# A fused attention and gated MLP kernel: the head and the first two chunks rewritten as one listed order

## The chip, the core and the metric

The kernel runs on one core of one Trainium2 chip. Its time is the device time of one execution in microseconds (us). Before the change it is 250.87 us, the median of three runs (250.81 to 252.08). The engines are called as in the profile: PE (matrix multiply), PEld (its weight loads), DVE (vector), ACT (activations), POOL and SP; POOL and SP also issue transfers (DMA).

## What is computed

Four batches of eight heads, 768 positions, 64 values a head. The positions form eight blocks of 96. A small matrix per head is normalized five times by rows and columns (Sinkhorn) and mixes the blocks of k and v; attention then runs inside each block, and its result goes through an MLP with the gate h cos h.

```python
P = sort_net
for _ in range(5):
    P = P - np.max(P, axis=-1, keepdims=True)
    P = np.exp(P)
    P = P / (np.sum(P, axis=-1, keepdims=True) + 1e-09)
    P = P / (np.sum(P, axis=-2, keepdims=True) + 1e-09)
k_sorted = np.einsum('bhij,bhjcd->bhicd', P, k_b)
v_sorted = np.einsum('bhij,bhjcd->bhicd', P, v_b)
scores = scale * np.matmul(q_b, k_sb.transpose(0, 1, 2, 4, 3))
attn = softmax(scores)
x = np.matmul(attn, v_sb)          # (3072, 512) after reordering
h = x @ w_in                       # (3072, 2048)
out = (h * np.cos(h)) @ w_out      # (3072, 512)
```

## The kernel before

**Tiling.** The 3072 rows of the result are worked in eight chunks of 384 rows; chunk n holds half of batch n // 2, that is four blocks (u = 0 to 3). Sinkhorn works on two groups of two batches, one group in 128 partitions. Batches 0 and 1 make up group 0.

**Steps of a chunk.** Each block goes through `qk` (eight score matmuls into one PSUM tile, then a maximum, L454, and a subtraction, L455, on DVE), `expo` (L479 on ACT), a transpose of the probabilities p (`p_transpose`, L503 on PE, or by DMA from SP's queue, L490), `av` (eight matmuls, L516, a reciprocal and a product on DVE, L523 and L525) and `x_transpose` (L541). Then `moe_up` runs eight `up` calls (16 feature tiles of 128, L553, cosine on ACT L557, gate product on DVE L560), and `moe_down` runs three row tiles of 16 matmuls each into an accumulator (L570), copies them out and stores them. Score groups, sorts and transposes of the following chunk are placed in slots between these calls, written out by hand for each chunk.

**Sorting.** k and v are multiplied on PE by a block-diagonal matrix made from Sinkhorn's result (`bd`, spread at L274). `k_sort_0` sorts batch 0 for one half of its blocks, `k_sort_1` batch 1. `v_sort_b` needs v with the value index outermost; half of batch 0's columns are read straight from the loaded tile `kv`, the others after a permuting copy on POOL (`v_permute`, L177) into `vperm`.

**Memories.** PSUM has two pools: "big" with three tiles of two banks (B in the code) and "acc" with two tiles of one bank (C). Every score, sort, up and down result needs one of these tiles and holds it until ACT or DVE has read it.

**Order.** Each engine works its instructions in the order in which the code writes them. POOL's queue carries all loads of q, k, v and the weights beside memsets and permutes; SP's queue carries the small swaps of k halves (`k_swap`), transposes by DMA and most stores. Before, the head runs like this: sort_net is loaded; q for chunk 0, k and v of batch 0 are requested (L195 to L197); both Sinkhorn groups run in step for four iterations (L311 to L337), with chunk 0's query transposes and three weight loads between them; then batch 0's first half is sorted and chunk 0's four blocks are worked (L609 to L636). Chunk 0's up pass runs in two halves of 192 rows (L651 to L659). Batch 0's second half and batch 1 are sorted in slots of chunk 0's up and down passes and of chunk 1's up pass. From chunk 1's down pass on (L702) the work is the same in both versions.

**Keeping the PE busy.** `keep_warm` (L216) issues matmuls on a zero tile of 256 columns whose result nobody reads: 16 at the start, then three at a time between Sinkhorn steps.

Of the kernel before, what the change touches and what calls it, by code (L numbers as in the profile page):

```python
# [10 lines left out]
FP32 = mybir.dt.float32  # L11
# [3 lines left out]
AX = mybir.AxisListType  # L15


@with_exitstack
def kernel(
# [42 lines left out]
    gp = ctx.enter_context(tc.tile_pool(name="gp", bufs=9))  # L62
# [14 lines left out]
    ident = const.tile([128, 128], BF16, name="ident")  # L77

# [22 lines left out]
    QR, NQ = 4, 3  # L101

    QZ = IC * H2 * 2 * D
    q_mem = const.tile([blk, 2 * (QZ + D)], BF16, name="q_mem")
    q_rows = q_mem[:, :H * QR * D].rearrange("p (h x) -> p h x", h=H)
# [10 lines left out]

    def load_q(n):  # L120
        b, ih = n // 2, n % 2
        if n < NQ:

            nc.gpsimd.dma_start(
                out=q_rows, in_=q[b][:, ih * IC * blk:(ih + 1) * IC * blk].rearrange(
                    "h (p r) d -> p h (r d)", r=QR))
# [40 lines left out]
    def v_permute(rows, lo=0, halves=True):  # L167

        for z in range(lo, D, VQ):
            dst = vperm[rows, :CD].rearrange("p (d c) -> p d c", d=D)[:, z:z + VQ]
            src = vv[rows, z:z + VQ, :blk]
            if halves:
                dst = dst.rearrange("p d (x t) -> p d x t", x=2)
                src = src.rearrange("p d (t x) -> p d x t", x=2)
            nc.gpsimd.tensor_copy(dst, src)  # L177

# [7 lines left out]
    kT, kT2 = [kTs[:, :, 0], kTs[:, :, 2]], kTs[:, :, :2]  # L186

    make_identity(nc, ident[:])
    NP = 3
    p_bufs = []  # L190
    for i in range(NP):
        t = const.tile([blk, 2 * H2, 128], BF16, name=f"p_buf{i}")
        nc.gpsimd.memset(t[:, :, blk:], 0.0)
        p_bufs.append(t)
    load_q(0)  # L195
    load(kbuf, 64, kin_d[0])
    load(vbuf, 0, vin_d[0])  # L197
# [6 lines left out]
    ones(0)  # L204
# [3 lines left out]
    warm = const.tile([128, 128], BF16, name="warm")  # L208
    nc.vector.memset(warm[:], 0.0)
    nc.vector.memset(vperm[:, CD:], 0.0)  # L210
    nc.vector.memset(kbuf[:64, :32 * D], 0.0)
# [16 lines left out]
    L = [const.tile([128, 2 * H, nb], FP32, name=f"L{g}") for g in range(NG)]  # L228
# [5 lines left out]

    for g in range(NG):
        nc.vector.reduce_max(nmx[g][:], P_a[:, g], axis=AX.X, negate=True)
        nc.scalar.activation(
            E[g][:], P_a[:, g], AF.Exp, bias=nmx[g][:], accum_out=cs[g][:])
# [13 lines left out]
    def product(lhs, rhs):  # L252
        ps = acc.tile([128, nb], FP32, name="sk", tag="acc")
        nc.tensor.matmul(
            ps[:], lhs.rearrange("p x j -> p (x j)"), rhs[:], start=True, stop=True)
        return ps

    for g in range(NG):
        nc.vector.reciprocal(ci[g][:], cs[g][:])
        nc.vector.scalar_tensor_tensor(  # L260
            L[g][:], rows_of, ci[g][:], along(E[g]), op0=ALU.mult, op1=ALU.mult)
    sk = [product(L[g], maskj) for g in range(NG)]
    keep_warm(3)
    nc.vector.tensor_copy(same[:], rows_of)
    nc.vector.tensor_copy(
        maskp.rearrange("p (b e x) -> p b e x", b=2, e=2),
        maskh.rearrange("p (b x e) -> p b e x", b=2, e=2))
# [18 lines left out]
    def q_turn(n, z, pool, tag):  # L286

        ps = pool.tile([128, 2, IC, QR, blk // QR], BF16, name="qps", tag=tag)  # L290
        for e in range(2):
            for hp in range(2):
                for r in range(QR):
                    nc.tensor.transpose(
                        ps[hp * D:(hp + 1) * D, e, :, r],
                        q_rows[:, (z * 2 + e) * 2 + hp, r * D:(r + 1) * D], ident[:blk, :blk])

        def place(hp, rows):
            dst = q_of(n, hp)[rows, :QW].rearrange("d (i h c) -> d h i c", h=H2, c=blk)
            return dst[:, z * 2:z * 2 + 2], ps[rows].rearrange("d e i r p -> d e i (r p)")  # L300

        if n == 0:
            return [place(0, slice(0, 128))]
        return [place(hp, slice(hp * D, (hp + 1) * D)) for hp in range(2)]

    def q_transpose(n, z, engs, pool, tag):
        for eng, (dst, src) in zip(engs, q_turn(n, z, pool, tag)):
            copy_on(eng, dst, src)

    held = const.tile([128, 1], FP32, name="held")  # L310
    for it in range(4):  # L311
        for g in range(NG):
            nc.scalar.activation(E[g][:], T[g][:], AF.Exp, scale=ci[g][:])
        if it > 1:
            copy_on(A, *turned[0])
        sk = [product(same, E[g]) for g in range(NG)]
        if it in (1, 2):
            turned = q_turn(0, it - 1, big, "big")
        keep_warm((3, 0, 0, 3)[it])
        if it == 1:  # L320

            nc.gpsimd.tensor_copy(held[:], cs[1][:])
            for z in range(3):
                load_w_in(z)
            v_permute(slice(0, 64), D // 2, False)
        elif it == 2:
            load_w_in(3)
            load_q(1)
            for z in range(4):
                load_w_out(z)  # L330
        for g in range(NG):
            nc.vector.reciprocal(rr[g][:], sk[g][:])
            nc.vector.tensor_tensor_reduce(
                T[g][:], E[g][:], rr[g][:], 1.0, 1e-9, ALU.mult, ALU.add, cs[g][:])
            nc.vector.reciprocal(ci[g][:], cs[g][:])
            if it == 3:
                spread(g)  # L337

    nc.vector.tensor_copy(
        order.rearrange("k (p r) -> k p r", r=QR),  # L340
        ident[:blk, :blk].rearrange("k (r p) -> k p r", r=QR))

    MH = H2 * IC
# [5 lines left out]
    def k_sort_0(ih, t0, nt, eng, pool, tag):  # L349

        ps = pool.tile([128, nt, 2 * MH], FP32, name="ks", tag=tag)
# [3 lines left out]
        ms, ts = slice(ih * MH, (ih + 1) * MH), slice(t0, t0 + nt)  # L355
        psv = ps.rearrange("p t (e m) -> p e m t", e=2)
        for hp in range(2):
            for x in range(2):
                copy_on(eng, kT[0][hp * D:(hp + 1) * D, hp + x, ms, ts],
                        psv[x * D:(x + 1) * D, hp])  # L360

    def k_sort_1(t0, eng, pool, tag):
        ps = pool.tile([128, 8, 2 * NB], FP32, name="ks", tag=tag)
# [3 lines left out]
        copy_on(eng, kT[1][:, ::2, :, t0:t0 + 8], ps.rearrange("p t (e m) -> p e m t", e=2))  # L367

    def k_sort_g(t0, eng, pool, tag):
        ps = pool.tile([128, 4, 4 * NB], FP32, name="ks", tag=tag)  # L370
# [10 lines left out]

    def keys_of(n, u, h2, hp):
        g, b2, ih = where(n)
        z = slice(hp, hp + 2)
        if n < 2:
            return kT[0][:, z, ih * MH + h2 * IC + u]
        m = h2 * nb + ih * IC + u
        return kT[1][:, z, m] if g == 0 else kT2[:, z, b2, m]

    def scores(out, n, u, h2, hp):  # L390
        x = (u * H2 + h2) * blk
        if n == 0:
            rows = slice(hp * D, (hp + 1) * D)
            nc.tensor.matmul(
                out[:blk], q_of(0, 0)[rows, x:x + blk], keys_of(n, u, h2, hp)[rows],
                start=True, stop=True)
        else:

            nc.tensor.matmul(  # L399
                out, q_of(n, hp)[:, x:x + 128], keys_of(n, u, h2, hp), start=True, stop=True)  # L400


    bdv = const.tile([128, 2 * H, nb], BF16, name="bdv")

    def v_turn():
        ps = big.tile([128, 128], FP32, name="bdp", tag="big")
# [4 lines left out]
        nc.scalar.copy(bdv.rearrange("p x i -> p (x i)"), ps[:])  # L411

    def v_cols(d, permuted):
        return vperm[:, d * blk:d * blk + 128] if permuted else vv[:, d]

    def v_sort_b(b, d0, nd, eng, pool, tag):
        ps = pool.tile([128, nd, 2 * NB], FP32, name="vs", tag=tag)


        rows, xs = slice(0, 64 + b * 64), slice((1 - b) * H, (2 - b) * H)  # L420
        for t in range(nd):
            nc.tensor.matmul(  # L422
                ps[:, t], v_cols(d0 + t, b == 1 or d0 + t >= D // 2)[rows],
                bdv[rows, xs].rearrange("p x i -> p (x i)"), start=True, stop=True)
        copy_on(
            eng, vS[0][:, b * 2 * NB:(b + 1) * 2 * NB, d0:d0 + nd],
            ps[:blk].rearrange("p t n -> p n t"))

    def v_sort_g(d0, nd, eng, pool, tag):
        ps = pool.tile([128, nd, 4 * NB], FP32, name="vs", tag=tag)  # L430
# [15 lines left out]
    def qk_part(n, u, part, pool, tag):  # L446
# [360 lines left out]
```

## Time and profile before

| What | Value |
|---|---|
| time, median of three runs (lowest to highest) | 250.87 us (250.81 to 252.08) |
| span of the profiled execution, first to last instruction | 248.0 us |
| PE busy | 231.1 us (93%) |
| DVE busy | 175.8 us (71%) |
| ACT busy | 157.3 us (63%) |
| POOL busy | 88.2 us (36%) |
| mean granted PE clock | 0.945 |
| sorting matrix of group 0 starts being spread | 12.66 us |
| first up matmul (chunk 0) | 29.20 us |
| first down matmul (chunk 0) | 51.96 us |
| first up matmul of chunk 1 | 70.72 us |
| HBM read, written | 27.27 MB, 6.29 MB |

The profiled execution's own time is not listed; the span stands for it, and what lies around the span is taken from the median time. Times inside the profile count from the start of the span. "Busy" of PE covers the whole flight of a matmul, so that a PE that is busy all the time need not be at its peak. The granted clock is the share of full speed that the chip's throttle lets the PE have at that time. In a listing by group, "idle before" names what ended the wait ahead of an instruction. A stage table gives busy time of each engine in a stretch of time, the number of instructions in brackets, then clock, share of the DMA engines and GB/s.

### The profile page before, as it was taken

The page shows a single profiled execution, that of the slowest core. Times are in us where ns is not written, and L with a number is a line of the kernel's source. Part 1 is how long each engine was busy: PE and PEld are TensorE (multiplying, and loading weights), DVE is VectorE, ACT ScalarE, POOL GpSimd, SP SyncE. Part 2 cuts the span into 40 slices and gives each one's busy share as a digit, 9 for nine tenths or more (in the row PEclk, how much of TensorE's full clock was granted, in tenths as well). Part 3 has the DMA queues.
Part 4 walks back from the last instruction along what each step waited for, and adds up shares of the span by engine and source line. Part 5 has one row for each costly group of instructions (what it writes and reads, how often), then busy time and mean ns, then how long its engine had stood idle before and what let it go on. Part 6 is the DMA issues. An engine that isn't in the chain of part 4 may idle for free.

```text
span 248.0 us, 5329 instructions
## 1 busy us (share of the span) xinstructions
PE 231.1 (93%) x2131; PEld 148.7 (60%) x2151; DVE 175.8 (71%) x322; ACT 157.3 (63%) x224; POOL 88.2 (36%) x104
## 2 busy tenths in 40 slices
PE   7887798878999999999999999999999999979994
PEld 5776696745566656665666556655565556435543
DVE  5579558897478876688568997898789759524710
ACT  4467846676568975789568866684667456634710
POOL 6369990799879707110353500800000000000000
PEclk9655569999999999999999999999999999999999
DMA  5999999895997058846897978937651650371012
GB/s 55 232 193 174 197 201 231 134 213 105 181 233 130 6 137 110 136 110 148 172 102 134 59 184 151 158 39 181 153 110 32 176 114 0 97 119 42 0 43 86
DMA packets 69001, 31.49 MB, mean 127 GB/s; under 512 B 57840, under 2 KB 64496, under 8 KB 68720
## 3 DMA queue, kind: packets, MB, share of 16 engines
q0 software_dynamic: 24048, 13.64, 40.8%
q1 hardware_dynamic: 43408, 15.28, 27.2%
q10 hardware_dynamic: 1520, 2.24, 2.8%
q8 instruction: 17, 0.28, 0.5%
q14 instruction: 8, 0.07, 0.1%
HBM read 27.27 MB, written 6.29 MB: 135 GB/s over the span
## 4 chain that ended last, share of the span: by engine, by line
PE 75%; DVE 10%; ACT 6%; DMA 5%; issue 2%; ACTq 0%; DVEq 0%; SPq 0%
PE h L553 32%; PE o L570 24%; PE sc L399 3%; PE av L516 3%; DMA vperm<-p_buf 2%; PE pps L503 2%; ACT p_buf L479 2%; DVE kTs L282 2%; PE ks L346 2%; PE vs L432 1%; DVE gg L560 1%; PE o L771 1%; DVE xn L525 1%; PE vs L422 1%; PE xps L541 1%
## 5 line engine op out<-in xcount | busy, mean ns | idle before, releaser
L553 PE MATMUL h<-xT,w_in_t 128*128 128x384 bf16 (+1 forms) x576 | 93.3, 313 | 2.1 <-DVE gg L560 0.8
L570 PE MATMUL o<-w_out_t,gg 128*128 128x512 bf16 x348 | 84.0, 379 | 1.6 <-DVE s L455 0.5
L557 ACT ACTIVATE c<-h,half_pi 128x768 f32<-128x768 f32 (+1 forms) x72 | 59.7, 830 | 36.2 <-PE h L553 33.9
L560 DVE TENSOR_TENSOR gg<-c,h 128x768 bf16<-128x768 f32 (+1 forms) x72 | 61.3, 859 | 25.2 <-ACT c L557 25.1
L553 PEld LDWEIGHTS <-w_in_t 128*128 128x128 bf16 x576 | 53.8, 100 | 29.7 <-issue 2.9
L570 PEld LDWEIGHTS <-gg 128*128 128x128 bf16 x368 | 33.6, 98 | 33.6 <-DVE s L455 0.7
L454 DVE TENSOR_REDUCE mx<-sc 96x4 f32<-96x384 f32 (+1 forms) x43 | 31.9, 741 | 3.2 <-PE sc L399 2.3
L455 DVE TENSOR_TENSOR s<-sc,mx 96x384 f32<-96x384 f32 (+1 forms) x43 | 32.2, 749 | 2.3
L177 POOL COPY vperm<-kv 64x1536 bf16<-64x1536 bf16 (+1 forms) x10 | 28.2, 2841 | 6.2 <-DMA kv<-in_v_dram 5.2
L479 ACT ACTIVATE p_buf<-s 96x768 bf16<-96x768 f32 x32 | 27.6, 894 | 2.4 <-ACT o_s L280 1.0
L280 ACT COPY o_s<-o 128x512 f32<-128x512 f32 (+1 forms) x18 | 10.3, 573 | 25.0 <-PE o L570 23.8
L525 DVE TENSOR_TENSOR xn<-av,r 96x512 bf16<-96x512 f32 x32 | 22.0, 686 | 1.1
L280 ACT CAST kTs<-ks 128x512 bf16<-128x512 f32 (+2 forms) x31 | 14.1, 456 | 6.2 <-PE ks L346 6.0
L134 POOL DMA_DIRECT2D kv<-in_q_dram x24 | 16.0, 675 | 3.1 <-DMA kv<-in_v_dram 2.2
L399 PE MATMUL sc<-kTs,q_turned 128*128 128x96 bf16 x224 | 16.1, 206 | 0.9 <-DVE s L455 0.7
L523 DVE RECIPROCAL r<-av 96x8 f32<-96x8 f32 x32 | 6.4, 199 | 14.7 <-PE av L516 14.6
L399 PEld LDWEIGHTS <-q_turned 128*128 128x128 bf16 x224 | 12.8, 98 | 4.8 <-DVE s L455 1.3
L282 DVE COPY o_s<-o 128x512 f32<-128x512 f32 (+1 forms) x7 | 4.5, 647 | 12.1 <-PE o L771 8.6
L557 ACT ACT_TABLE_LOAD x8 | 10.3, 1283 | 0.9 <-ACT o_s L280 0.7
L134 POOL DMA_DIRECT2D q_mem<-in_q_dram x16 | 10.6, 675 | 0.3 <-issue 0.3
L280 ACT CAST pair<-vs 96x512 bf16<-96x512 f32 (+1 forms) x12 | 8.7, 728 | 2.5 <-PE vs L432 2.0
L516 PEld LDWEIGHTS <-pT 96*128 96x128 bf16 (+1 forms) x160 | 7.8, 106 | 3.4 <-issue 1.2
(96 smaller groups left out, 212.8 us busy)
## 6 DMA issues: line engine op xcount, KB each, us to landing
out_dram<-o_s SPq DMA_DIRECT2D x15, 256.0 KB, 2.6
w_in_t<-in_moe_w_in_dram POOLq DMA_DIRECT2D x4, 512.0 KB, 10.6
w_out_t<-in_moe_w_out_dram POOLq DMA_DIRECT2D x4, 512.0 KB, 12.9
out_dram<-o_s ACTq DMA_DIRECT2D x8, 256.0 KB, 2.5
kv<-in_k_dram POOLq DMA_DIRECT2D x2, 768.0 KB, 13.3
kv<-in_v_dram POOLq DMA_DIRECT2D x2, 768.0 KB, 16.5
pair<-in_k_dram POOLq DMA_DIRECT2D x2, 768.0 KB, 11.5
kv<-in_v_dram POOLq DMA_DIRECT2D x6, 256.0 KB, 6.2
```

The source lines that it names most:

```text
L134: nc.gpsimd.dma_start(out=q_heads[:, i, :, e], in_=src[:, ih * IC + i, :, e])
L177: nc.gpsimd.tensor_copy(dst, src)
L280: eng.copy(dst, src)
L399: nc.tensor.matmul(out, q_of(n, hp)[:, x:x + 128], keys_of(n, u, h2, hp), start=True, stop=True)
L454: nc.vector.reduce_max(mx[:], scv, axis=AX.X)
L455: nc.vector.tensor_tensor(s_t[n, u][:, part[0]:part[0] + w], scv, mx.to_broadcast([blk, w, H2, blk]), op=ALU.subtract)
L479: nc.scalar.activation(dst, src, AF.Exp, scale=scale)
L525: nc.vector.tensor_tensor(xn.rearrange("p h e d -> p e h d"), avv[:, :, :, :D], r.to_broadcast([blk, 2, H2, D]), op=ALU.mult)
L553: nc.tensor.matmul(h[:, f2, :w], w_in_t[:, kk, f * 128:(f + 1) * 128], xT[n][:, kk, lo:hi], start=(kk == 0), stop=(kk == KC - 1))
L557: nc.scalar.activation(c[:, :, :w], h[:, :, :w], AF.Sin, bias=half_pi[:, 0:1])
L560: nc.vector.tensor_tensor(gt[n, fp][:, :, lo:hi], c[:, :, :w], h[:, :, :w], op=ALU.mult)
L570: nc.tensor.matmul(o[:], gt[n, f // 2][:, f % 2, ts * 128:(ts + 1) * 128], w_out_t[:, f, :], start=(f == 0), stop=(f == FC - 1))
```

## The change

Everything from the first load to the end of chunk 1's up pass is now one list of short calls (`ORDER`), worked from left to right; each call issues one step on one engine. The helpers are split so that a matmul group, its maximum, its subtraction or its eviction are calls of their own (`qm`, `qx`, `qs`; `vm`, `vc`; `um`, `uc`, `ug`; `dm`, `do`; `am`, `an`; `pp`, `pc`; `xt`, `xc`; `qt`, `qc`). The letter behind a call names the pool (B, C) or the engine (V for DVE, A for ACT, S for SP). `w` n puts n filler matmuls ahead of the next PSUM tile's own matmuls.

- q of both chunks of batch 0, k and v of batches 0 and 1 are requested ahead of all weights; q comes in halves (`load_q_half`), with two positions a piece in place of four, and chunk 1's q goes into the tile `pair`.
- Group 0's Sinkhorn iterations (`se`, `sp`, `sv` with second number 0) run ahead of group 1's, whose last two iterations move behind chunk 0's scores.
- Chunk 0's queries are transposed to both row halves: 64 transposes in place of 32. Its scores are 16 matmuls of 64 x 48 a block (one for each half of the keys) in place of eight of 64 x 96, and the sorted keys are written by three copies of 128 lanes (`k0c`) in place of sixteen of 64.
- Batch 0's second half of keys (`k4`, with a swap by DMA, `sw4`) and batch 1's keys (`k1`) are sorted in the head, ahead of and among chunk 0's scores.
- POOL's memsets and permutes stand between the weight loads (`zq1`, `one`, `zv`, `pv`).
- Chunk 0's up pass works four feature tiles of 192 rows in one PSUM tile, so that cosine and gate run on 768 elements instead of 384. Gate tiles hold two up calls each (five tiles in place of nine).
- Chunk 1's probabilities are transposed by DMA (`pd`), chunk 0's by PE.
- Fillers: 16 at the start as before, then 1, 6, 8, 8 and 3.

```diff
+ORDER = """
+se 0 0, sp 0 0, sv 0 0, se 1 0, lq 0 1, lk0, qt 0 0 0 2, qt 0 0 2 4, w 1, qt 0 0 4 6,
+qt 0 0 6 8, sp 1 0, qc 0 0 0 V, sv 1 0, se 2 0, qc 0 0 1 V, od, se 0 1, qt 0 1 0 8, sp 2 0,
+sv 2 0, qc 0 1 0 A, se 3 0, sp 0 1, lk1, sv 0 1, w 6, sp 3 0, w 8, se 1 1, qc 0 1 1 A, lv0,
+lq 1 1, sv 3 0, spr 0, lv1, lq 1 0, sp 1 1, k0 0 4 16 16 B, sv 1 1, k0c 0 4 16 16 A,
+k0 0 4 32 16 B, k0 0 4 0 16 B, k0c 0 4 32 16 A, se 2 1, k4 0 C, k1 32 B, k1 24 C,
+k0c 0 4 0 16 V, qm 0 0, k4c 0 A, k1 16 C, k1c 24 A, k1c 32 V, wi 0, wi 1, wi 2, wi 3, zq1,
+one 0, wo 0, zv, k1 8 C, k1 40 B, qx 0 0, qs 0 0, k1c 16 A, wo 1, qm 0 1, qx 0 1, qs 0 1,
+pv 0 2, pv 0 3, wo 2, pv 1 3, pv 1 2, wo 3, k1c 40 A, k1c 8 A, ex 0 0, k4 32 C, k4 16 C,
+vt, vtc A, k4c 32 A, k4c 16 A, qm 0 2, w 8, vm 0 0 8 24 8 C, qt 1 1 0 8, ex 0 1,
...
+vm 0 0 8 32 8 C, qc 1 1 0 V, qx 0 3, qs 0 3, vm 0 0 8 56 8 C, pp 0 0 B, w 3,
+vm 0 0 8 48 8 B, vm 0 0 8 40 8 B, pc 0 0 V, vc 0 0 8 48 8 V, pp 0 2 B, vc 0 0 8 32 8 A,
+vc 0 0 8 56 8 A, vc 0 0 8 40 8 A, pp 0 1 C, am 0 0, pc 0 2 V, ex 0 3, am 0 2, pc 0 1 A,
+an 0 0, an 0 2, sw4, pp 0 3 B, vm 1 0 8 48 8 C, pc 0 3 A, vc 1 0 8 48 8 A, am 0 1, k1 0 C,
+k1c 0 A, an 0 1, qm 1 3, qt 1 0 0 8, xt 0 2 C, qx 1 3, qs 1 3, xt 0 1 C, xc 0 2 A,
+xc 0 1 A, xt 0 0 C, am 0 3, sp 2 1, lk2 1, xc 0 0 A, vm 1 0 8 40 8 C, qm 1 2, sv 2 1,
+an 0 3, qx 1 2, qs 1 2, lk2 0, zp 0, zp 1, zp 2, pv 1 1, pv 1 0, lv2 3, lq 2 1, lv2 1,
+lv2 5, lv2 4, qc 1 0 0 V, lv2 2, qc 1 0 1 A, um 0 4 0 192, vc 1 0 8 40 8 A, se 3 1, ex 1 3,
+um 0 0 0 192, sp 3 1, vm 1 0 8 32 8 C, uc 0 4 0 192, um 0 2 0 192, vc 1 0 8 32 8 A, sv 3 1,
...
+do 0 2 V S, qh 2 0 0, um 1 0, uc 1 0, um 1 1, uc 1 1, ug 1 0, ug 1 1, spr 1, um 1 5,
+uc 1 5, ug 1 5, qh 2 0 1, qh 2 1 0, qh 2 1 1
+"""
...
+    def space(pool, shape, name, dtype=FP32):
+        pool, tag, banks = {"B": (big, "big", 2), "C": (acc, "acc", 1)}[pool]
+        if dtype == BF16 or not fill[0]:
+            return pool.tile(shape, dtype, name=name, tag=tag)
+
+        n = math.prod(shape[1:])
+        flat = pool.tile([128, 512 * banks], FP32, name=name, tag=tag)
+        for _ in range(fill[0]):
+            nc.tensor.matmul(flat[:, :256], warm[:], warm[:, :1].to_broadcast([128, 256]),
+                             start=True, stop=True)
...
+    def k0_mm(i0, ni, t0, nt, pool):
+        ps = ks[0, i0, t0] = space(pool, [128, nt, ni * H], "ks")
         for t in range(nt):
             k_products(ps, t, t0 + t, slice(64, 128),
-                       bds[0][64:, H:, ih * IC:(ih + 1) * IC])
...
+    def k0_out(i0, ni, t0, nt, eng):
+        copy_on(eng, kT0[:, 0, i0 * H:(i0 + ni) * H, t0:t0 + nt],
+                ks.pop((0, i0, t0)).rearrange("p t m -> p m t"))
...
+        qf = q_turned[n][:, u // U2]
+        for j in range(H):
+            w = (u % U2 * H + j % H2 * 2 + j // H2) * blk
+            for x in range(2):
+                rows = slice(x * D, (x + 1) * D)
+                nc.tensor.matmul(
+                    sc[:, x, j * HT:(j + 1) * HT], qf[rows, w:w + 128],
+                    kT0[rows, n, u * H + j], start=True, stop=True)
...
+    def up_mm(n, fp, lo=0, hi=TC):
+
+        w = hi - lo
+        z = TC // w
+        h = h_t[n, fp, lo] = space("B", [128, 2, 512], "h")
+        for f2 in range(2 * z):
+            f = fp * 2 + f2
+            for kk in range(KC):
+                nc.tensor.matmul(
+                    h[:, f2 // z, f2 % z * w:(f2 % z + 1) * w],
+                    w_in_t[:, kk, f * 128:(f + 1) * 128], xT[n][:, kk, lo:hi],
+                    start=(kk == 0), stop=(kk == KC - 1))
...
+    for call in ORDER.replace("\n", " ").split(","):
+        name, *args = call.split()
+        calls[name](*(named[a] if a in named else int(a) if a.isdigit() else a for a in args))
```

More of the change, by code (lines that the diff above doesn't have):

```diff
@@ L165, with v_permute @@
     VQ = 16
[L167 to L177, printed above, removed]
+    def v_permute(b, z):
+        rows = slice(b * 64, b * 64 + 64)
+        dst = vperm[rows, :CD].rearrange("p (d c) -> p d c", d=D)[:, z * VQ:(z + 1) * VQ]
+        src = vv[rows, z * VQ:(z + 1) * VQ, :blk]
+        if b:
+            dst = dst.rearrange("p d (x t) -> p d x t", x=2)
+            src = src.rearrange("p d (t x) -> p d x t", x=2)
+        nc.gpsimd.tensor_copy(dst, src)
     HT = blk // 2
     kTs = const.tile([128, 3, 3, NB, HT], BF16, name="kTs")
-    kT, kT2 = [kTs[:, :, 0], kTs[:, :, 2]], kTs[:, :, :2]
+    kT0, kTm, kT1, kT2 = kTs[:, :2, 0], kTs[:, :, 1], kTs[:, :, 2], kTs[:, :, :2]
+    load_q_half(0, 0)
     make_identity(nc, ident[:])
     NP = 3
[L190 to L197, printed above, removed]
+    p_bufs = [const.tile([blk, 2 * H2, 128], BF16, name=f"p_buf{i}") for i in range(NP)]
     vS[0] = const.tile([blk, 4 * NB, VW], BF16, name="vS")
@@ L339, with q_turn @@
[L339 to L343, printed above, removed]
+    q_ps = {}
+    def q_turn(n, a, h0=0, h1=H):
+        if h0 == 0:
+            q_ps[n, a] = q_space(n)
+        ps = q_ps[n, a]
+        for h in range(h0, h1):
+            for r in range(QR):
+                src = q_rows(n)[:, a, h, r * D:(r + 1) * D]
+                for z in range(2) if n == 0 else (h % 2,):
+                    nc.tensor.transpose(
+                        ps[z * D:(z + 1) * D, h // H2, h % H2, :, r] if n == 0 else
+                        ps[z * D:(z + 1) * D, 0, h // 2, :, r], src,
+                        ident[:blk, :blk])
@@ new lines, in q_space, with q_place @@
+    def q_space(n):
+        ps = space("B", [128, H // H2 if n == 0 else 1, 1024], "qps", BF16)
+        return ps[:, :, :H2 * U2 * blk].rearrange(
+            "d b (h i r p) -> d b h i r p", h=H2, i=U2, r=QR)
+    def q_place(n, a, part, eng):
+        ps = q_ps[n, a]
+        if n == 0:
+            dst = q_turned[n][:, a, :QW].rearrange(
+                "d (i b h c) -> d b h i c", b=2, h=H2, c=blk)
+            copy_on(eng, dst[:, part], ps[:, part].rearrange("d h i r p -> d h i (r p)"))
+            return
+        rows = slice(part * D, (part + 1) * D)
+        dst = q_of(n, part)[rows, :QW].rearrange("d (i h c) -> d h i c", h=H2, c=blk)
+        copy_on(eng, dst[:, :, a * U2:(a + 1) * U2],
+                ps[rows, 0].rearrange("d h i r p -> d h i (r p)"))
@@ L444, with qk_part @@
     cnt = [0]
[L446 removed]
+    def qk_part(n, u, part, pool):
         w = len(part)
[L448 removed]
+        sc = space(pool, [128, w, 512], "sc")
         for h2 in range(H2):
@@ L660, with hold_sort, no_pad, no_other @@
-    load_q(2)
-    for z in range(2):
+    def hold_sort(g):
+        nc.gpsimd.tensor_copy(held[:], cs[g][:])
+    def no_pad(z):
+        nc.gpsimd.memset(p_bufs[z][:, :, blk:], 0.0)
+    def no_other():
+        nc.gpsimd.memset(q_turned[0][64:, 0], 0.0)
+        nc.gpsimd.memset(q_turned[0][:64, 1], 0.0)
+    def no_first():
+        nc.gpsimd.memset(vperm[:64, :VP * blk], 0.0)
+    def no_other_1():
+        nc.gpsimd.memset(q_turned[1][64:, 0], 0.0)
+        nc.gpsimd.memset(q_turned[1][:64, 1], 0.0)
```

474 lines of the change are left out of this document (248 added, 226 removed).

## The prediction

> **What bounds the kernel now.** First the page's busy slices: PE is at nine tenths from slice 10 on, and its gaps lie ahead of that, where the granted clock is low as well.
>
> ```profile
> PE   7887798878999999999999999999999999979994
> ...
> POOL 6369990799879707110353500800000000000000
> PEclk9655569999999999999999999999999999999999
> ```
>
> Second, the busy times of three stages, cut where the first up matmul starts (29.20) and where chunk 1's down pass starts (83.95). Columns: start and end, length, then busy time and count of PE, PEld, DVE, ACT, POOL, then granted clock, DMA share and GB/s.
>
> ```profile
> 0.00:29.20 29.20, 23.29 (x264) 18.79 (x265) 21.02 (x77) 18.96 (x40) 20.92 (x32) 0.63 1.02 168
> 29.20:83.95 54.75, 50.28 (x630) 37.11 (x633) 40.01 (x74) 36.12 (x59) 43.19 (x36) 0.95 0.97 169
> 83.95:248.00 164.05, 157.49 (x1240) 92.77 (x1254) 114.78 (x172) 102.19 (x127) 24.09 (x38) 1.00 0.57 106
> ```
>
> The third stage is PE at full clock, and the change leaves it as it is. So everything hangs on when chunk 1's down pass starts; I call that time S. Third, the chain of waits: sorting matrix ready, first av, first up, and S itself.
>
> ```profile
> 12.66 0.35 DVE bd L274
> ...
> 25.73 0.64 PE av L516 x8
> ...
> 29.20 1.44 PE h L553 x8
> ...
> 83.78 0.17 PE sc L399 x4
> 83.95 0.21 PE o L570
> ```
>
> Fourth, POOL's timeline: the two permutes of batch 0's v wait for that load (14.64), and memsets follow later.
>
> ```profile
> 14.64 5.48 POOL L177 COPY vperm<-kv 64x1536 bf16<-64x1536 bf16 x2 [4.69 <-DMA kv<-in_v_dram]
> ...
> 25.70 1.40 POOL L642 MEMSET q_turned<- 64x1568 bf16 x1
> ...
> 34.66 2.65 POOL L649 MEMSET vperm<- 64x3072 bf16 x1
> ```
>
> Fifth, the granted clock by the microsecond. It falls at 7.9 and comes back at 35.05, after four microseconds with PE busy 1.00; at 50 it stands at 1.00 with PE busy only 0.56.
>
> ```profile
> 7.00:8.00 1.00, 0.39 (x2) 0.30 (x2) 0.57 (x6) 0.54 (x2) 0.47 (x2) 0.89 0.93 197
> 8.00:9.00 1.00, 0.89 (x12) 0.87 (x14) 0.67 (x5) 0.32 (x2) 1.00 (x2) 0.50 0.93 197
> 34.00:35.00 1.00, 1.00 (x15) 0.92 (x14) 0.23 (x1) 0.49 (x1) 0.93 (x4) 0.50 1.25 205
> 35.00:36.00 1.00, 1.00 (x24) 0.97 (x23) 0.84 (x3) 0.59 (x3) 1.00 (x1) 0.95 1.24 205
> ...
> 50.00:51.00 1.00, 0.56 (x9) 0.56 (x10) 1.00 (x3) 0.36 (x1) 1.00 (x1) 1.00 1.04 209
> ```
>
> The span is 248.0. The profiled execution's own time isn't listed beside it, so I take the median, 250.87, for it: 2.87 lie around the span.
>
> **The change, part by part.** The work ahead of S is the same in kind (both chunks' ups, chunk 0's down, both batches' sorts, four half score groups of chunk 2); its order is new.
>
> *Sinkhorn.* Group 0 goes alone. One of its iterations takes 1.6 unhindered (7.14 to 8.74 on ACT), against 2.1 when queries were turned in between (8.74 to 10.88). It can start 0.2 sooner, since the two copies ahead of T (0.14 and 0.08 at 4.94) now come before the load. From 5.3, four iterations and the 0.35 spread give 12.0 instead of 13.0. There are 64 query transposes in place of 32 (0.79 for 16 at clock 0.50, 0.83 for 32 at 1.00); each half's 32 lie beside the 1.2 of DVE and ACT in an iteration, so they cost 0 to 0.4 each.
>
> *Loads.* POOL issues two query halves, k0, k1 and v0 in a row. The first three loads of before, 1.97 MB, were in at 14.64. k1 now stands where v0 stood, and the first issue is some 1.3 earlier (0.75 instead of 2.02): 13.4. v0 is 0.79 MB further; at 0.22 MB/us (197 to 246 GB/s between 7 and 13) 16.9.
>
> *POOL.* Its queue is in order: the last w_in issue waits for k1 (one of eight loads must have landed): 13.4 + 0.77, two memsets of 1.40, ones 0.72 = 17.7; then a w_out issue 0.77, the vperm memset 2.65, another issue 0.77, two permutes 5.48 = 27.4. Before, these permutes ended at 20.1. This is what chunk 0's av now waits for.
>
> *Ahead of 27.4.* k sorts, chunk 0's scores and the plain v sorts lie beside POOL. PE's rows for them sum to some 14 at full clock. Scores take 16 matmuls of 64x48 a group instead of 8 of 64x96; no row shows 48 columns: between the 64x32 sort (0.03) and the 64x96 score (0.058), 0.5 to 0.9 a group against 0.46; I take 0.5, hidden either way. Query halves come in 512-byte pieces: a whole chunk landed in 5.1 to 7.8, a half takes between half of that and all of it; at worst Sinkhorn starts 2.5 late, of which PE's slack (12.0 + 14 against 27.4) hides 1.4. ACT's list up to the first up sums to 18 from 12, also covered.
>
> *27.4 to the first up.* 24 v-sort matmuls (0.72), three transposes of p (0.37 each), three fillers (0.4), av 0.26: 29.9. Then DVE's list: three normalizations (0.20 + 0.69), a 96x768 max and subtract (1.87), a Sinkhorn step (0.75), a fourth normalization: 36.1, against 29.20 before. ACT's evictions fit beside it. The key swap for chunk 1 (landing 7.4 to 7.8) issues near 19.5 and is needed at 31.6, cover 4.
>
> *First up to the last.* PE's list at full clock: 128 up matmuls of 192 (0.097 each, 12.4), 64 of 384 (0.1625, 10.4), 48 down (0.216, 10.4), v sorts 1.4, scores 0.85, av 1.05, x transposes 0.85, query transposes 0.85, Sinkhorn 0.4: 38.6. The second up waits 0.35 for chunk 1's next subtract; banks and hand-overs add 1.6 by my walk through the list (some 20 hand-overs at 0.04, the rest bank waits). Cosines now come in eight of 768 (0.90) instead of sixteen of 384 (0.58), gates in eight of 0.95 instead of sixteen of 0.55; ACT and DVE sum to 31 and 35 in this stretch and are no bound. Weights landed by 33 (w_in) and 43 (w_out) at 0.2 MB/us. The end of the last up: 76.6.
>
> *A new wait at S.* Three half score groups now stand behind the last up. They share two banks with the first down output, which waits for the second one's subtract: ACT 0.90, DVE 0.95, twice (0.55 + 0.55), and DVE's backlog: 4.4. Before, the last scores ended at 83.95 and down followed at once. Sum: S = 81.0.
>
> Costed at nothing: larger gate buffers (five of double size), L in the cosine pool, pad memsets moved into POOL's later queue, batch 1's permutes (end 41.4, last user 46), p transposes by DMA on SP's queue (2.6 each, from 37 and 49 on; last user 59; the first output store stands behind them and nobody waits for it). If that cover is gone, each late transpose delays PE one to one.
>
> Forecast: 81.0 + 164.05 + 2.87 = **247.9**.
>
> **The rivals.** *The clock* (slower). Between 24.8 and 27.4 PE waits for POOL with nearly nothing to do. Against a fall: 32 transposes stand in 4.5 to 7.9, where before had six fillers, and 14 fillers follow; at 50 the clock held with PE at 0.56. For it: before lost the clock at 7.9 with PE nominally at 0.39 to 0.98 and won it back only after a full stretch. At 0.50 the rows behind 27.4 are p transposes 0.88, av 0.64, v sorts 0.46: first up at 41 instead of 36.1, and the first two ups 0.18 a matmul, another 2.6: S = 88.5, time 255.4. It decides from 3 us of added PE time on; a fall for the middle only gives 252 to 253.
> [...]
> *The waits close up* (faster): v0 earlier, or bank waits and half of S's new wait hidden by PE running late: 36.1 + 38.6 + 2 = 76.7, time 243.6. PE at 0.99 in the third stage speaks for dense lists, the ups of before at 49 to 52 (PE 0.74, 0.56, 0.49, DVE 0.97 to 1.00) against it.
> *POOL later still*: every microsecond beyond 27.4 moves the first up by one; three make it no gain: 250.9. The permutes' rows (2.75 to 2.89) scatter little.
> *It doesn't do what it says*: ups start at 29 as before, because something other than POOL releases av; then time falls further, and the first up shows it. I count it with the faster rival.
>
> **How the numbers follow.** Under 0.5% (1.25 us) this kernel's measurement can't tell from no change. Chances: forecast 0.42 (245 to 250.5, a fifth of it within 1.25 of 250.87), waits close up 0.18, clock 0.28 (252 to 256), POOL later 0.12 (half even, half slower). Faster 0.34 + 0.18 = 0.52, same 0.08 + 0.06 = 0.14, slower 0.28 + 0.06 = 0.34. The likeliest case's own range is 245 to 250.5; to hold 8 in 10 the range takes in most of both sides, 243 to 256.
>
> **What would show it.** Batch 0's last permute ending near 27.4; first up near 36; granted clock 1.00 from 5 to 36; PE without gaps of over 1 us from 36 to 76; a PE gap of about 4 ahead of chunk 1's down pass; S near 81. Wrong if the clock shows 0.50 behind 28, if the first up is behind 40, or if the stage behind S isn't 164.

## The result, and the profile after

The changed kernel is slower: 268.84 us median of 4 runs (267.46 to 270.11), beside 250.97 for the kernel before in the same measurement; the ratio is 1.071, with a 95% interval of 1.065 to 1.077. The profiled execution took 268.77, its span is 267.0 (1.77 lie around it). The forecast was 247.9, the range 243 to 256. A ratio below is against the kernel before, measured beside each kernel; runs that lie over 1.5% above their kernel's fastest (two of four in e2, one of four in e7 and in e11) are left out of it.

The busy slices (6.7 us each) show three dents in PE behind 40 us (4, 5 and 4 tenths, at 40, 67 and 93) that the kernel before has not, and four stretches of low granted clock instead of one:

```profile
PE   7998994899589949999999999899999979999995
...
POOL 8459968754330791160008070070000000000000
PEclk9655559799959977999999999999999999999999
```

The same three stages as before the change, cut at the first up matmul (46.15) and at chunk 1's down pass, S (99.04). Columns: start and end, length, busy time and count of PE, PEld, DVE, ACT, POOL, granted clock, DMA share, GB/s.

```profile
0.00:46.15 46.15, 39.24 (x538) 33.74 (x539) 27.36 (x79) 22.21 (x43) 34.84 (x37) 0.67 1.11 189
46.15:99.04 52.89, 42.82 (x402) 29.78 (x407) 30.48 (x49) 31.75 (x40) 26.98 (x27) 0.89 0.92 122
99.04:267.00 167.96, 159.90 (x1239) 93.86 (x1256) 113.72 (x170) 99.51 (x124) 25.10 (x38) 0.98 0.58 103
```

The first stage is 16.95 longer than before, the second 1.86 shorter, the third 3.9 longer. So what was to be gained behind the first up was mostly not there, and what was to be paid ahead of it was more than twice the forecast. The chain of waits names what stands in the first two stages (start, length, what):

```profile
10.82 1.31 PE sk L131 x6
...
12.36 1.72 PE sk L131 x8
...
14.30 4.37 PE ks L393 x80
...
23.33 1.87 PE vs L131 x8
...
36.91 0.93 PE av L626 x16
...
42.43 2.55 DVE T L383
...
51.05 11.28 DMA pT<-p_buf
...
62.60 11.53 DMA pT<-p_buf
```

L131 are the fillers. From 14.3 to the first av (36.71) the chain is PE, but for 3.4 on ACT: POOL's permutes, on which the forecast hung this stretch, are not in it. They end at 30.2, and PE reaches the first sort that reads them only at 31.62 (timelines of POOL and PE):

```profile
24.66 5.53 POOL L242 COPY vperm<-kv 64x1536 bf16<-64x1536 bf16 x2
```

```profile
31.62 0.61 PE L481 MATMUL vs<-bdv,vperm 64*128 64x64 bf16 x8
```

Then come a DVE step that takes 2.55, and two transposes of p by DMA of 11 us each. PE's timeline shows the waits that follow from these, and the one ahead of S (the time idle is in brackets, with what ended it):

```profile
46.15 4.40 PE L686 MATMUL h<-xT,w_in_t 128*128 128x192 bf16 x32 [3.25 <-DVE xn L638]
...
71.38 0.43 PE L626 MATMUL av<-vS,pT 96*128 96x65 bf16 x8 [1.61 <-DMA pT<-p_buf]
74.18 0.65 PE L626 MATMUL av<-vS,pT 96*128 96x65 bf16 x8 [2.37 <-DMA pT<-p_buf]
...
97.99 0.50 PE L454 MATMUL sc<-kTs,q_turned 128*128 128x96 bf16 x4 [3.16 <-DVE s L516]
```

The granted clock stands at 0.50 in the head up to 39, and goes back to it behind each of these three pauses (0.52, 0.50 and 0.50), as the rows of two microseconds show (granted clock is the third number from the end); 32 up matmuls at 46.15 take 4.40, where 32 in a row take 2.80 later:

```profile
14.00:16.00 2.00, 2.00 (x33) 1.98 (x32) 0.55 (x4) 0.59 (x1) 0.00 (x0) 0.50 1.00 209
...
39.00:41.00 2.00, 1.88 (x47) 1.63 (x45) 1.71 (x4) 1.57 (x4) 0.26 (x1) 0.94 1.24 208
46.00:48.00 2.00, 1.85 (x12) 1.74 (x13) 1.90 (x4) 0.00 (x0) 1.70 (x2) 0.52 1.15 219
...
75.00:77.00 2.00, 1.96 (x14) 1.11 (x14) 0.75 (x2) 0.43 (x1) 0.87 (x1) 0.50 1.54 181
...
99.00:101.00 2.00, 1.74 (x4) 0.72 (x6) 1.00 (x2) 0.84 (x1) 2.00 (x1) 0.50 0.44 98
```

```profile
61.25 2.80 PE L686 MATMUL h<-xT,w_in_t 128*128 128x192 bf16 x32
```

### The profile page after: what moved, and what is told of

Its sections match the earlier page's. It is cut to its first block, busy times and chain, and to the rows that moved or that the text cites. A ratio compares the mean times of both kernels' runs of the same rounds, so it can differ in the third digit from the quotient of the medians.

```text
span 267.0 us, 5393 instructions
## 1 busy us (share of the span) xinstructions
PE 242.0 (91%) x2179; PEld 157.4 (59%) x2200; DVE 171.6 (64%) x296; ACT 153.5 (57%) x207; POOL 86.9 (33%) x100
## 4 chain that ended last, share of the span: by engine, by line
PE 63%; DMA 19%; DVE 8%; ACT 5%; issue 2%; SPq 0%; POOL 0%; ACTq 0%; DVEq 0%; POOLq 0%
PE h L686 24%; PE o L720 19%; DMA pT<-p_buf 12%; PE ks L393 3%; DMA vperm<-p_buf 3%; PE av L626 3%; PE vs L481 3%; DMA q_mem<-in_q_dram 2%; PE sc L454 2%; DVE gg L702 2%; ACT p_buf L584 2%; DMA kTs<-kTs 1%; PE o L899 1%; DVE s L516 1%; PE qps L351 1%
## 5 line engine op out<-in xcount | busy, mean ns | idle before, releaser
L720 PE MATMUL o<-w_out_t,gg 128*128 128x512 bf16 x347 | 87.9, 392 | 2.1 <-issue 0.6
L702 DVE TENSOR_TENSOR gg<-c,h 128x768 bf16<-128x768 f32 x64 | 60.0, 949 | 26.8 <-ACT c L693 26.7
L693 ACT ACTIVATE c<-h,half_pi 128x768 f32<-128x768 f32 x64 | 57.5, 902 | 30.1 <-PE h L686 28.3
L515 DVE TENSOR_REDUCE mx<-sc 96x4 f32<-96x384 f32 (+1 forms) x33 | 24.0, 729 | 5.2 <-PE sc L454 5.2
L516 DVE TENSOR_TENSOR s<-sc,mx 96x384 f32<-96x384 f32 (+1 forms) x33 | 24.3, 736 | 1.8
L335 ACT CAST kTs<-ks 128x512 bf16<-128x512 f32 x22 | 12.6, 584 | 10.9 <-PE ks L393 10.9
L242 POOL COPY vperm<-kv 64x1536 bf16<-64x1536 bf16 x6 | 16.5, 2786 | 0.1
L626 PE MATMUL av<-vS,pT 96*128 96x65 bf16 (+1 forms) x128 | 7.4, 212 | 5.0 <-DMA pT<-p_buf 4.5
L335 ACT CAST vS<-vs 96x512 bf16<-96x512 f32 x14 | 7.9, 594 | 6.6 <-PE vs L481 6.6
L826 POOL COPY vperm<-kv 128x1536 bf16<-128x1536 bf16 x4 | 11.2, 2870 | 0.1
## 6 DMA issues: line engine op xcount, KB each, us to landing
kv<-in_v_dram POOLq DMA_DIRECT2D x6, 256.0 KB, 14.3
```

The source lines that it names most:

```text
L335: eng.copy(dst, src)
L515: nc.vector.reduce_max(mx[:], scv, axis=AX.X)
L516: nc.vector.tensor_tensor(s_t[n, u][:, part[0]:part[0] + w], scv, mx.to_broadcast([blk, w, H2, blk]), op=ALU.subtract)
L626: nc.tensor.matmul(a[:w, hp, h2 * (D + 1):(h2 + 1) * (D + 1)], pt[:blk, e * blk:e * blk + w], vS[g][:, v_at(g, b2, hp, h2, ih * IC + u), : ...
L693: nc.scalar.activation(c[:], h_t[n, fp, lo][:, :, :TC], AF.Sin, bias=half_pi[:, 0:1])
L702: nc.vector.tensor_tensor(dst.rearrange("p (y z) w -> p y z w", z=z), c_t.pop((n, fp, lo)).rearrange("p y (z w) -> p y z w", z=z), h_t.pop ...
```

## The experiments

My theory after the two traces: no single wait but five causes one behind the other. They are PE's own list at half rate ahead of the first av (with fillers and slow weight loads in it), a DVE step held up by POOL, DMA transposes held up by loads, the wait at S, and a fall of PE's rate behind each pause. The main rival: one cause (POOL, or the rate alone), behind which the rest follows. The table gives the marks in each trace, in us; the trace of e2, an execution of 267.59 us and above its median, is not in it.

| kernel | first av | first up | last up ends | S | behind S | ratio (95%) |
|---|---|---|---|---|---|---|
| before | 25.73 | 29.20 | 83.79 | 83.95 | 164.05 | 1 |
| changed | 36.71 | 46.15 | 94.48 | 99.04 | 167.96 | 1.071 (1.065 to 1.077) |
| e1 | 37.03 | 47.03 | 91.77 | 96.30 | 170.30 | 1.067 (1.061 to 1.073) |
| e3 | 38.40 | 45.67 | 95.95 | 108.93 | 166.77 | 1.109 (1.104 to 1.113) |
| e4 | 34.59 | 44.61 | 91.45 | 96.00 | 168.30 | 1.063 (1.059 to 1.068) |
| e5 | 34.65 | 44.01 | 92.05 | 96.58 | 167.92 | 1.063 (1.057 to 1.069) |
| e6 | 37.03 | 44.43 | 92.29 | 96.81 | 167.89 | 1.059 (1.053 to 1.065) |
| e7 | 31.36 | 40.42 | 88.70 | 89.56 | 170.64 | 1.047 (1.042 to 1.053) |
| e8 | 31.35 | 39.31 | 85.21 | 86.07 | 169.53 | 1.024 (1.018 to 1.030) |
| e9 | 31.67 | 39.41 | 84.47 | 85.34 | 167.86 | 1.016 (1.009 to 1.023) |
| e10 | 33.45 | 41.41 | 86.48 | 87.35 | 166.35 | 1.014 (1.008 to 1.020) |
| e11 | 37.19 | 47.49 | 93.58 | 98.12 | 166.28 | 1.059 (1.051 to 1.068) |

**e1, p transposes on PE.**

```
- pd 1 3, pd 1 2, pd 1 1, pd 1 0
+ pp 1 3 C, pc 1 3 A   (and the same for 1 2, 1 1, 1 0 in pool B)
```

> Chunk 1's four p transposes on PE with copies on ACT, instead of by DMA on SP's queue; all else as in the changed kernel. Theory T (the DMA transposes, 11 us each, hold up av of chunk 1): the two PE waits at 71.4 and 74.2 (4.0 together, 1.6 more ahead of them) and the clock fall behind them (half clock from 73.7 to 80.1, about 3.1 of lost work) go, 1.5 of PE turns is added: S about 99 - 8.7 + 1.5 = 92, time 261 to 263. Rival R (what is late is set before the first up, and the waits only move): S stays at 97 to 99 and the time at 267 to 269.

The result lies between the two in S and, at 267.1 us, with R in the time. The waits for the transposes are gone, and from the first up to S it takes 49.3 instead of 52.9; but PE now waits 2.0 for a copy on ACT, the first up is 0.9 later, and the stage behind S is 2.3 longer, so that the fall of the time (0.4%) is within the intervals. This trace shows something else. Its clock column says 1.00 where that of the changed kernel says 0.50, and the same matmuls take the same time. First e1, then the changed kernel:

```profile
26.00:28.00 2.00, 2.00 (x24) 1.82 (x25) 0.21 (x1) 1.01 (x2) 2.00 (x2) 1.00 1.24 206
```

```profile
26.00:28.00 2.00, 2.00 (x24) 1.82 (x25) 0.53 (x1) 1.32 (x2) 2.00 (x2) 0.50 1.24 217
```

Eight fillers take 1.86 in e1 (at 23.65) and 1.87 in the changed kernel (at 23.33), where sixteen take 1.94 at full rate (e10): PE ran at half rate in both, and e1's record lacks the first fall. Such gaps in the record would also explain why the four runs of the changed kernel have mean clocks of 0.911, 0.968, 0.942 and 0.968 within 1% of one time. The rate is to be read from the length of a known matmul.

**e2, the half score groups spread.**

```
- lq 2 1 / qt 2 1 ahead of lq 2 0 / qt 2 0
+ lq 2 0 / qt 2 0 ahead of lq 2 1 / qt 2 1
- do 0 2 V S, qh 2 0 0, um 1 0, ... ug 1 5, qh 2 0 1, qh 2 1 0, qh 2 1 1
+ ug 1 3, qh 2 0 0, ... ug 1 4, qh 2 0 1, ... ug 1 7, qh 2 1 0, ... um 1 1, qh 2 1 1
```

> Only the seam ahead of chunk 1's down pass: the rows of chunk 2's first half are loaded and turned first, and the four half score groups stand between the last ups instead of three behind the last one. Theory N (the new wait at S, 3.7 of PE idle, also lets the clock fall from 97.5 to 104): S 3 to 4 earlier and the stage behind S back from 168 to 165, time 261 to 263. Rival B (DVE is full in these last ups, so that the wait only moves ahead): under 1.5 us faster, stage behind S still 167 to 168.

The ratio is 1.050 (1.041 to 1.060), the lowest of a single edit, though its interval meets those of e4, e5, e6 and e11. It rests on two runs (261.3 and 264.6 us); the median of all four is 265.8. Chunk 1's last stage of ups, from its first 384-wide one to S, takes 14.2 instead of 16.7, in this trace and again in e8, e9 and e10: PE's wait there falls from 3.7 to 0.9. So the seam's 2.5 are shown, less than the 3 to 4 of N. Whether the stage behind S becomes shorter too, as N says, e2 leaves open: in its one trace S comes only 1.0 earlier, and 167.8 follow it.

**e3, the loads held back.**

```
- lk2 1, lk2 0, lv2 ..., lq 2 1, lq 2 0 at their places
+ pd 1 0, ph 1 0, lk2 1, lk2 0, lq 2 1, lq 2 0, lv2 ...    (ph: POOL reads the transposed p)
```

> The loads of batches 2 and 3 (k, v) and of chunk 2's queries are issued only when chunk 1's last p transpose by DMA has landed. Theory L (the transposes take 11 us because they share the DMA engines with these loads): each lands in 3 to 5 us, PE's waits for them at 71 and 74 go; what then is late are the loads, by up to 10 us. Rival Q (they are slow because four stand on one queue, whatever else runs): they still take 9 to 12 us each. The time itself tells little here, since the loads come late; I expect 262 to 272.

Theory L holds: the four transposes land in 2.6 to 4.3 (median 3.6) instead of 10.1 to 11.5. The time, 277.5 us, is above the 262 to 272 that were expected. The last one in the chain of e3:

```profile
64.39 2.62 DMA pT<-p_buf
```

PE is through with the work ahead of chunk 2's first query turn at 73.7, in the changed kernel at 81.9. The gain is given back: 6.1 waiting for the late queries, and 11.6 for a DVE operation that stood beside POOL's late permutes (timelines of DVE and POOL in e3):

```profile
96.57 9.33 DVE L329 SCALAR_TENSOR_TENSOR bd<-maskp,ci,T 128x128 bf16<-128x128 f32 x1
```

```profile
94.85 10.91 POOL L826 COPY vperm<-kv 128x1536 bf16<-128x1536 bf16 x4
```

It ends at 105.90, the last of the four permutes at 105.76. In the changed kernel the same operation took 0.38, and the same four permutes ran there too; it began just ahead of the end of the second (90.19 + 2 x 2.81 = 95.81) and came in between two of them:

```profile
95.64 0.38 DVE L329 SCALAR_TENSOR_TENSOR bd<-maskp,ci,T 128x128 bf16<-128x128 f32 x1
```

```profile
90.19 11.23 POOL L826 COPY vperm<-kv 128x1536 bf16<-128x1536 bf16 x4
```

**e4, no fillers.** The calls `w 1, w 6, w 8, w 8, w 3` are left out.

> The 26 filler matmuls inside the order (1, 6, 8, 8 and 3) are left out; the 16 at the start stay. Theory F (at half clock they only delay: 1.31 + 1.72 + 1.87 + 0.64 of the chain to the first up): the sorting matrix is ready 2 to 3 us earlier and the first up comes at 42 to 44 instead of 46.15, time 264 to 267. Rival K (they bring the clock back): the clock comes back later than 39, the first up no earlier than 46, time 268 or more.

Theory F holds in kind: the first av comes 2.1 earlier and the first up 1.5, and rival K is out. Its sizes were too large: the sorting matrix is ready 0.2 earlier, not 2 to 3, and the first up at 44.61 lies above the expected 42 to 44. PE now waits 1.4 for POOL's permutes, so the two lists had been nearly level (PE's timeline in e4):

```profile
30.97 0.60 PE L480 MATMUL vs<-bdv,vperm 64*128 64x64 bf16 x8 [1.38 <-POOL vperm L241]
```

**e5, wide weight loads.**

```
- return vperm[:, d * blk:d * blk + 128] if permuted else vv[:, d, :blk]
+ return vperm[:, d * blk:d * blk + 128] if permuted else vv[:, d]
```

> Only the 32 plain v sorts: their weight load reads 128 columns of v again, as before the change, instead of 96. Theory W (the 96-column load takes 0.17 against 0.10 and sets these matmuls' pace, 0.18 each against 0.117): the 32 take 3.7 instead of 5.8, and since PE is busy without a pause from 14.3 to the first av, that comes 1.5 to 2 us earlier, at about 35; time 266.5 to 268. Rival C (they are slow because PE runs at half rate there, whatever the width): still 0.18 each, first av at 36.7.

Theory W holds. The weight loads of the changed kernel and of e5 (groups from 3 to 60; busy time, mean ns):

```profile
L481 PEld LDWEIGHTS <-kv 64*96 64x96 bf16 x32 | 5.4, 252 | 0.5 <-issue 0.4
```

```profile
L480 PEld LDWEIGHTS <-kv 64*128 64x128 bf16 x32 | 3.1, 211 | 0.5 <-issue 0.4
```

That is 0.169 against 0.097 a load, and PE's 32 matmuls take 3.4 instead of 5.8; the first av is 2.06 earlier, nearly all of the 2.4 that PE's list lost.

**e6, POOL's permutes behind the DVE step.**

```
- zp 2, pv 1 1, pv 1 0
+ zp 2, hs 1, pv 1 1, pv 1 0     (hs: POOL reads the step's sum)
```

> POOL's second pair of permutes (v of batch 1, columns 0 to 31) waits for Sinkhorn's step on DVE (it reads that step's sum first), so that the two no longer run beside each other. Theory P (a POOL permute holds up this DVE operation, 2.55 instead of 0.17, until the permute in progress ends): the operation takes 0.17, PE's idle time ahead of the first up falls from 3.25 to about 0.9, the first up comes at 43.8, and since the pause is short PE doesn't fall to half rate behind it (first 32 matmuls 3.1 instead of 4.4): last up 3 to 4 earlier, time 264 to 267. Rival D (the operation is late for a reason of its own): still 2.5, first up 46.

Theory P holds in the step, in PE's wait (0.78) and in the rate behind it; the last up comes only 2.2 earlier, not 3 to 4, since PE waits for the DMA transposes as before (2.32 and 1.60). The step in e6, and the up matmuls that follow, at full rate:

```profile
43.09 0.17 DVE L382 CUSTOM_DVE_ANT_0 T<-E,rr 128x8 f32<-128x8 f32 x1
```

```profile
44.43 1.48 PE L685 MATMUL h<-xT,w_in_t 128*128 128x192 bf16 x16 [0.78 <-DVE xn L637]
46.35 1.48 PE L685 MATMUL h<-xT,w_in_t 128*128 128x192 bf16 x16 [0.44 <-DVE s L554]
```

In the changed kernel the same operation began 0.24 behind the start of a permute and ended with it: 42.43 + 2.55 = 44.98, and of the two permutes, 5.47 together, the first ends near 44.9.

```profile
42.19 5.47 POOL L242 COPY vperm<-kv 64x1536 bf16<-64x1536 bf16 x2
```

That the rate holds because the pause is short is not shown by e6 alone. The same 0.78 stands ahead of the first up in e8, with full rate behind it (1.48 for 16), and in e9 and e10, with half rate (4.42 and 4.46 for 32). PE's timeline in e9:

```profile
39.41 4.42 PE L686 MATMUL h<-xT,w_in_t 128*128 128x192 bf16 x32 [0.78 <-DVE xn L638]
```

**e7 and e8, everything together,** e7 with the transposes by DMA and batch 3's v held back, e8 with e1's transposes on PE.

> All causes found so far taken away together, with the p transposes of chunk 1 still by DMA: no fillers in the order, 128-column loads for the plain v sorts, batch 0's permutes ahead of two w_out loads and a memset, the second pair of permutes behind Sinkhorn's step, half score groups spread between the last ups, and the loads of batch 3's v issued only when the last p transpose has landed (chunk 2's queries ahead of it). If the theory of several separate delays is complete: first av at 31 to 32, first up at 39 to 41, S at 81 to 84, time 248 to 251. Rival (the order itself is too long, each delay removed shows the next one): S at 88 or more, time over 255.

> As e7, but chunk 1's p transposes on PE with copies on ACT, and the loads as in the changed kernel. PE gets 1.5 and ACT 3.2 more: if the loads no longer hurt anything, 1 to 2 slower than e7, time 249 to 253; if the held loads in e7 are late for what follows, faster than e7.

e7's first up came as expected, but S at 89.6, on the rival's side: the held loads push POOL's memsets of q_turned and its permutes later, PE waits 2.6 for the first and 2.6 for a DVE operation beside the second. e8 stands better, with S at 86.1, but its 257.1 us miss the expected 249 to 253. e8 differs from e7 in two things, the transposes and the loads; which of them helped was not taken apart.

**e9, one copy on DVE.** `pc 1 3 A` becomes `pc 1 3 V`.

> As e8, but the copy behind the first p transpose of chunk 1 on DVE instead of ACT. In e8 PE waited 2.0 for that copy, which stood behind a table load of 1.28 and an exponential on ACT. If that wait was on the path: time 254.5 to 256; if ACT's later list sets the pace anyway: 257 as e8.

The time is 255.08 (254.87 to 255.34), as expected if the wait was on the path. The marks bear out a part of it: S comes 0.7 earlier, and the stage behind S, where the edit changes nothing, is 1.7 shorter; the intervals of e8 and e9 overlap. Of the 17.9 us that the change cost, 13.7 are gone and 4.2 are left. By the traces, S in e9 is 1.4 later than before the change and the stage behind it 3.8 longer (together 1.0 more than the medians say, since the trace of before is of a faster execution): most of what is left lies in the stage that the change does not touch.

**e10, a dense block of fillers.** `w 16` ahead of `sp 3 0` and again ahead of `se 1 1`.

> As e9, with two blocks of 16 fillers (128x256) ahead of and behind Sinkhorn's last sum, some 7 us of PE without a gap between 11 and 18. Theory G (the granted rate rises only after a long stretch of dense, wide matmuls; the 3 us of the change's own fillers were too few): the k sorts start 4 to 4.6 later, at 18.4, but a 64x64 v sort then takes 0.05 to 0.06 instead of 0.10 and a p transpose 0.045 instead of 0.107; first av at 27 to 29 instead of 31.35, first up at 34 to 36, time 250 to 253. Rival H (the rate doesn't follow fillers): the same durations as in e9 and everything 4 to 5 later: time 259 to 261.

Neither holds. The second 16 fillers take 1.94 and the first 3.57, so full rate was back when the second block began; but the k sorts behind hardly gain (4.00 instead of 4.43), and by 22 PE is at half rate again, though it shows next to no idle time (0.03 from 18 to 22). The k sorts can't tell the rate: 16 of 64x32 take 0.58 at a granted clock of 0.50 (changed kernel, 21.66) and 0.56 at 1.00 (kernel before, 39.35).

```profile
10.88 3.57 PE L131 MATMUL sk<-warm 128*128 128x256 bf16 x16
...
14.52 1.94 PE L131 MATMUL sk<-warm 128*128 128x256 bf16 x16
...
16.52 4.00 PE L393 MATMUL ks<-bd,kv 64*128 64x32 bf16 x80
```

```profile
18.00:20.00 2.00, 2.00 (x46) 1.97 (x44) 0.41 (x1) 1.06 (x4) 1.95 (x2) 1.00 1.44 190
20.00:22.00 2.00, 1.97 (x56) 1.73 (x54) 1.93 (x4) 1.73 (x3) 2.00 (x3) 0.83 1.14 213
22.00:24.00 2.00, 1.70 (x52) 1.46 (x50) 1.97 (x3) 1.86 (x3) 2.00 (x2) 0.50 1.20 167
```

The time is that of e9 within the intervals. S comes 2.0 later than in e9, which is the price of the block, and the stage behind S is 1.5 shorter; nothing shows that the block did that, as this stage scatters between the other kernels too (166.3 to 170.6).

**e11, POOL's order alone.**

```
- wi 3, zq1, one 0, wo 0, zv, ..., wo 1, ..., pv 0 2, pv 0 3, wo 2, pv 1 3, pv 1 2, wo 3
+ wi 3, zq1, one 0, ..., pv 0 2, pv 0 3, wo 0, wo 1, zv, pv 1 3, pv 1 2, wo 2, wo 3
```

> Only POOL's order is changed: batch 0's two permutes stand ahead of two w_out loads and the zeroing of vperm, so that they end at about 26 instead of 30.2. Step of the prediction (these permutes release the first av): first av 3 to 4 earlier, at about 33, time 264 to 266. Rival E (PE's own list from 14 on, at half rate, sets the first av): first av at 36 to 37 as before, time 267.5 to 269.5.

Rival E holds for the first av. The permutes end at 26.7 instead of 30.2, and the first av comes at 37.19 (PE's timeline in e11):

```profile
37.19 1.13 PE L625 MATMUL av<-vS,pT 96*128 96x65 bf16 x16
```

Its runs go from 264.5 to 273.7, so whether it is faster than the changed kernel by the 1% that the ratios suggest stays open; its first up and S give no reason for it (S is 0.9 earlier).

## Why the prediction was wrong, point by point

The forecast of S was 81.0, and it came at 99.04: 10.05 of the 18.0 ahead of the first up, 7.8 between it and the end of the last up, 0.2 at the seam. Then 3.9 behind S, and 1.1 less around the span: 247.9 + 18.0 + 3.9 - 1.1 = 268.7. In every run that lists both, 1.7 to 1.9 lie around the span; the 2.87 of the forecast came from setting the median beside the span of a faster execution.

- *Ahead of 27.4*: the step that failed first. "PE's rows for them sum to some 14 at full clock" and "beside POOL" made PE's list free, so that POOL's permutes released the first av. PE began at 14.2 instead of 12.0 and came to the first permuted sort at 31.62, 17.4 later; the permutes had ended at 30.2 (2.8 later than forecast, as the last w_in issue, POOL's twelfth load, waited for the fourth, k1, until 16.22 and not 13.4; it made no difference), and moving them to 26.7 left the first av where it was (e11). The 14 left out the eight fillers (1.87), and it took the plain v sorts for the rows of before, while they load 96 columns instead of 128 (2.4 of PE's time, 2.06 at the first av, e5). That last one is a line of the diff that I read past. These two are more than the 3.4 that were missing. The half rate shows behind 31.62: from there to the first av it took 5.1 where 2.2 were forecast from 27.4, with three p transposes at 2.39 instead of 1.11, three fillers at 0.84 instead of 0.4, and four groups of sorts in 2.2 where three in 0.72 were counted. No run had the full rate on that stretch, so what the half rate costs ahead of the first av is argued, not shown.
- *27.4 to the first up*: 6.5 were forecast from the start of the first av, 9.4 measured. "A Sinkhorn step (0.75)" had its price from before, where no permute ran beside it; beside one it took 2.55 for its second operation instead of 0.17 (e6). That permute is one of "batch 1's permutes", which were costed at nothing because of their own users; what they hold up was not asked. The order of the operations was as forecast.
- *First up to the last*: 40.5 forecast, 48.3 measured. "Costed at nothing: p transposes by DMA on SP's queue (2.6 each)" failed: 11.4 in the median beside the loads of batches 2 and 3, against 3.6 without them (e3). What I had put behind it, "each late transpose delays PE one to one", was right: 4.0 of waits. The half rate behind them costs some 2.9 more (from the last wait to chunk 2's query turn PE takes 7.7, and some 4.8 for the same list in e3), and that behind the pause ahead of the first up 1.6 (4.40 against 2.80). Together they are 8.5 of an excess of 7.8, so the sum of PE's list itself was about right.
- *A new wait at S*: right, in mechanism too; 4.4 forecast, 4.56 measured (94.48 to 99.04). Not seen was that the rate falls once more behind it (six down matmuls at 99.87 take 2.76, where eight at 86.08 took 1.89 before the change).
- *The stage behind S isn't touched*: wrong by 3.9. Chunk 1's down pass takes 16.75 up to the next up instead of 14.55, with PE at half rate up to 104; the next two down passes take 0.7 and 1.0 more, in waits for DMA transposes. In e8, where the rate holds behind S, that stage still takes 169.5: those waits are scattered (0.2 to 1.7 each in e8), lie at other places in other kernels, and what sets them was not tried. So this step stays open in part.
- *Sinkhorn*: group 0 was forecast at 12.0 and ready at 13.5; the second query half landed at 8.4, and PE's queue stood on its transposes.
- *The rivals*: the clock rival had sign and mechanism, at 255.4, but let the half rate count only behind 27.4, as the PE list ahead was taken to be hidden. "POOL later still" named the wrong engine. None had several causes at once, so the range ended 13 below the time. All three signs of being wrong came: 0.50 behind 28, the first up behind 40, the stage behind S not 164.

## What to carry to other kernels

Work that "lies beside" another engine is free only if its own list is shorter at the rate that the rows there show; so sum both lists, with fillers, before choosing which one releases the next step. When an order moves a step, look at what now runs beside it: a price from before held here only for the neighbours of before, for a DMA transpose (2.6 before, 11.4 beside the loads) as for an operation on DVE (0.17 before, 2.55 beside a permute). And a pause on PE can have a second price: here the half rate behind a wait of 3.25 cost another 1.6, and behind two waits of 4.0 together another 2.9.

## What the runs showed of the hardware

- The recorded clock is not proof of PE's rate: from 12 to 14 it read 1.00 in e1 and 0.50 in the changed kernel, over the same eight fillers, which took 1.87 in both; at full rate sixteen took 1.94 (e10).
- Beside a permute on POOL two DVE operations took longer, both of which read all their operands from SBUF. T<-E,rr took 0.17 in e6, without a permute beside it, and 2.55 to 2.65 in the changed kernel, e1, e2 and e4, where it began 0.14 to 0.24 behind the first of two permutes and ended within 0.1 of that one's end (taken as half of the pair); in e8 it took 0.95 and ended at 44.97, the pair at 44.94. bd<-maskp,ci,T took 0.35 in the head. Beside four permutes in a row its length differed: 0.38 in the changed kernel, begun just ahead of the end of one; 9.33 in e3, until the last of the four had ended (105.90 and 105.76). In e7 PE waited 2.65 for it, until 94.89, and the last of the four ended at 94.58. Why it came in between two permutes in the changed kernel and not in e3 was not tried. A reduction and a subtraction of scores in PSUM, at 45.92 and 46.97 beside the changed kernel's pair at 42.19, kept their 0.94 and 0.95.
- The weight loads of the 32 plain v sorts took 0.169 each with 96 columns (changed kernel) and 0.097 with 128 (e5).
- PE lost the full rate without a visible pause. In e10 sixteen 128x256 fillers, with 2 us of other matmuls right ahead, took 3.57, and the next sixteen 1.94. Behind k sorts and scores the rate fell again, with PE busy 2.00 and 1.97 of 2.00 from 18 to 22: 16 score matmuls of 64x48 took 0.37 at 20.45 and 0.50 at 22.04. In the changed kernel, behind 14 such fillers with sums between them (10.69 to 14.1) and behind the narrow sorts and transposes after them, the half rate stayed: eight fillers at 23.33 took 1.87, three at 33.66 took 0.84, and the clock read 0.50 until 39. What sets the rate was not tried.
- Between 20 and 125 us the traces list 14 waits of PE of 3.13 to 11.59 us, in the changed kernel, e1 to e6 and e11. Each was followed by half rate at once or within 1.1 us (behind 3.25 in the changed kernel 32 ups took 4.40, where 32 take 2.80 later). Behind shorter waits both were seen: full rate behind 2.62 in e7 (16 ups of 384 in 2.76), half rate behind 0.78 in e9 (32 ups of 192 in 4.42).
